# The seam between the MLP's last output product and the input-gradient product: a stated order of loads, and a first quarter with both halves over eight PSUM banks

## The chip, the cores and the metric

The kernel runs on one core of one Trainium2 chip. The metric is the time of one execution on the device in microseconds (us), the median of several runs. TensorE (PE in the profile) does the matrix products, VectorE (DVE) and ScalarE (ACT) the elementwise work, GpSimd (POOL) issues some of the DMAs and builds index tables, and SyncE (SP) issues most loads. [...] 

## The reference, cut to what matters

The forward pass is a conditioned mixer block, and the kernel returns its output and nine gradients for a given `grad_out`:

```
h = layernorm(x) * (1 + ca) + sa
x = x + ga * spectral(h)                  # rfft2, a learned filter, irfft2
h = layernorm(x) * (1 + cb) + sb
y = layernorm(h)
x = x + gb * (gelu(y @ w1 + b1) @ w2 + b2)
out, vjp = jax.vjp(forward, ...);  grads = vjp(grad_out)
```

There are S = 2048 tokens of D = 1024 features, and the MLP is F = 3584 wide; all inputs and outputs are bf16. With `ph` = (gb * grad_out) @ w2^T, the gradient at the MLP's hidden layer is `gz` = ph * gelu'(z), and the gradient at its input is gz @ w1^T. This last product is the one called the input-gradient product here. `sa` to `gb` are six rows of length D that come from `c` and `w_mod`; their gradients are sums over tokens, and the gradient of `w_mod` is an outer product of `silu(c)` with these sums.

## The kernel before, in words

The tokens are worked in NB = 4 blocks of BW = 512, and F in 7 groups g of 4 x 128 rows. The code is written as dataflow on named tiles. A scheduler puts the instructions of each engine in an order before the run, by priority and by when it reckons that tiles are free; `tc.issue_after(ins)` keeps an instruction behind `ins` in that order, `ordered()` keeps a PE instruction behind the PE instruction before it, and tiles with the same tag share a buffer, so that the later one waits for the earlier one's readers.

The stages around the change are these:

- `z_block(b, g0, g1)` (lines 782 to 817) computes z = y @ w1 (tile `pz`, L795), the gelu and its derivative, and stores `hh` (the activation) and `gz` to DRAM (L809, L817). It reads w1 from seven tiles with the tags `W1T`, and its temporaries `gt` take the tags t0 to t3.
- `bo_pass(b, h)` (L822) computes one half (512 of 1024 columns) of the MLP's output for block b in four PSUM banks `pbo`: a bias matmul each (L827), then 7 chunks of 16 matmuls (L836), each chunk against a slice of w2. The w2 slice is loaded by SP in the chunk's own program step (L831) into one of four buffers (w2sA, w2sC, w2sD, w2sB in turn). ACT then copies the banks out (L845), DVE multiplies and adds (L172, tile `otile`), the result is stored (L154, L159), and four narrow matmuls `pa` (L855) sum grad_out * output, which is added up in `gacc`.
- `plan` (L869 to 879) writes out the order of z blocks and bo chunks by hand. Blocks 0 to 2 have z blocks between the chunks; block 3 has none. The `pa` part of a pass is run one or two chunks into the next pass, and that of the last pass behind the loop (L898).
- Then come `pq` (L903), which finishes the sum in `gacc`, the store of its row (`store_gmod`, L178), and the gradient of b1 (`ptr`, L187, and L914).
- `gmod_ring` (L939) runs through w_mod row blocks with three buffers: load (L947), a product with sum (L958), a scaled row (L960), a store (L961). The instance `early` works on the row that `pq` made.
- `w1T_0` to `w1T_6` hold w1 transposed, 28 DMA transposes of 256 KB (L973) into the tags `W1T`. `gzr` are eight slots for gz (tags t0 to t3).
- The loop `for b in range(NB)` (L1001) does the input-gradient product: two halves h of 7 groups of 16 matmuls (`pg`, L1020) in four PSUM banks (`ps_f`), copied out by ACT with a running sum (L1025) into `gn3`. Then DVE takes the gradient through two layernorms (`ln_bwd`, L919 to 924; L1041), adds the residual, and folds the result for the spectral stage (`fold_tok`, `fold_d`, tiles n3u, pru, fbuf). `sums3` and `sums3_ga` (L195, banks `acc3a` and `acc3b`) add token sums on PE. The tile n3u is loaded once per block (L1005).
- Then the gradient of w2 begins (`gw2acc`, L1114); it needs four tiles `gB`, which take the buffers of w1T_0 to w1T_3 (load_tok, L127 and L130), and hh transposed from DRAM (`hht`, L1139).

Of the kernel before, what the change touches and what calls it, by code (L numbers as in the profile page):

```python
# [10 lines left out]
FP32 = mybir.dt.float32  # L11
BF16 = mybir.dt.bfloat16
I32 = mybir.dt.int32
ACT = mybir.ActivationFunctionType
# [3 lines left out]
P = 128  # L18
S = 2048
D = 1024  # L20
# [4 lines left out]
KH = D // 2  # L25
# [5 lines left out]
NB = 4  # L31
BW = S // NB
# [3 lines left out]
def kernel(  # L36
# [24 lines left out]
    nc = tc.nc  # L61
# [3 lines left out]
    small = ctx.enter_context(tc.tile_pool(name="small", bufs=2))  # L65
    reg = ctx.enter_context(tc.tile_pool(name="reg", bufs=1))
# [4 lines left out]
    W1T = PXT[2:6] + ["sma", "smb", "px0"]  # L71
# [7 lines left out]
    def ps_f(name):  # L79
        return psum.tile([P, 512], FP32, tag="f", name=name, bufs=4)  # L80
# [36 lines left out]
    d_gz_v = d_gz.rearrange("(fc p) s -> p fc s", p=P)  # L117
# [176 lines left out]
    wt = reg.tile([P, 2, NDC, 256], BF16, name="wt", tag="wt")  # L294
# [44 lines left out]
    for j in range(4):  # L339
        for cch in range(NDC):  # L340
# [326 lines left out]
    last_pe = [None]  # L667
# [80 lines left out]
    for g in range(7):  # L748
        wtile = reg.tile([P, NDC, BW], BF16, name=f"w1_{g}", tag=W1T[g])
# [11 lines left out]
    w2p = [uvp2[:, 1], reg.tile([P, 4, BW], BF16, name="w2sC", tag="gm")[:], px1t[:, 0]]  # L761
# [58 lines left out]
    w2n = [0]  # L820

    def bo_pass(b, h):  # L822
        cs_ = slice(h * KH, (h + 1) * KH)
# [2 lines left out]
            with ordered():  # L826
                last_pe[0] = nc.tensor.matmul(pbs[i][:], lhsT=ones_bf[0:1, :], rhs=b2_row[0:1, cs_], start=True, stop=False)  # L827
        for g in range(7):
            wp = w2p[w2n[0] % 4]
            w2n[0] += 1  # L830
            nc.sync.dma_start(out=wp, in_=w2_v[:, g * 4:(g + 1) * 4, cs_])  # L831
            hh = hh_slots[(b * 7 + g) % 11]
            for i in range(4):
                for k in range(4):
                    with ordered():
                        last_pe[0] = nc.tensor.matmul(pbs[i][:], lhsT=hh[:, k, i * P:(i + 1) * P], rhs=wp[:, k, :],  # L836
                                                      start=False, stop=(g == 6 and k == 3))
            if g < 6:
                yield
# [9 lines left out]
        store_tok_half(out_0, bo, b, h)  # L849

        yield
        pa = (ps_d if b < NB - 1 else ps_f)("pa")
        for i in range(4):
            with ordered():
                last_pe[0] = nc.tensor.matmul(pa[32 * i:32 * (i + 1), :], lhsT=ones_bf[:, 0:32], rhs=go[:, i, :], start=True, stop=True)  # L855
# [14 lines left out]
    bo_late = []  # L870
# [9 lines left out]
    for kind, b, g in plan:  # L880
# [7 lines left out]
        else:  # L888
# [6 lines left out]
                bo_late.clear()  # L895
            if g == 13:
                next(boq[b], None)
    for late in bo_late:  # L898
        next(late, None)
    g5 = []  # L900
    for h in range(2):
        pq = (ps_s, ps_d)[h]("pq")
# [62 lines left out]
                load_w(n + 2)  # L965
            yield

    w1Ts = []
    for g in range(7):
        wtile = reg.tile([P, 4, D], BF16, name=f"w1T_{g}", tag=W1T[g])  # L970
        for k in range(4):
            fc = g * 4 + k
            nc.sync.dma_start_transpose(out=wtile[:, k, :], in_=B_w1[:, fc * P:(fc + 1) * P])  # L973
        w1Ts.append(wtile)
    gzr = [reg.tile([P, 2, 4, BW], BF16, name=f"gzr{k}", tag=f"t{k}") for k in range(4)]
# [7 lines left out]
    gzn = 0  # L983
# [4 lines left out]
    au = reg.tile([P, 4, D], BF16, name="au", tag="px1")  # L988
# [9 lines left out]
    def sums3_ga(b, p4):  # L998
        halves_sum(acc3[1], p4, b == 0, b == 3)

    for b in range(NB):  # L1001
        gn3 = gn3s[b % 2]
        sums = small.tile([P, 2, 4], FP32, tag="sums")
        gzt = []
# [5 lines left out]
        for g in range(7):  # L1010
            sl = gzr[gzn % 8 // 2][:, gzn % 2]
            gzn += 1
            nc.sync.dma_start(out=sl, in_=d_gz_v[:, g * 4:(g + 1) * 4, b * BW:(b + 1) * BW])
            gzt.append(sl)
        for h in range(2):
            pgs = [ps_f("pg") for _ in range(4)]
            for g in range(7):
                for i in range(4):
                    for k in range(4):
                        nc.tensor.matmul(pgs[i][:], lhsT=gzt[g][:, k, i * P:(i + 1) * P],  # L1020
                                         rhs=w1Ts[g][:, k, h * KH:(h + 1) * KH],
                                         start=(g == 0 and k == 0), stop=(g == 6 and k == 3))
            for i in range(4):
                with tc.high_priority():
                    nc.scalar.activation(out=gn3[:, i, h * KH:(h + 1) * KH], in_=pgs[i][:], func=ACT.Identity,  # L1025
                                         accum_out=sums[:, h, i:i + 1])
        tt(sums[:, 0, :], sums[:, 0, :], sums[:, 1, :], ALU.add)
        for i in range(4):
            t = 4 * b + i
# [9 lines left out]
        for i in range(4):  # L1039
            t = 4 * b + i  # L1040
# [240 lines left out]
```

## Time and profile before

| what | value |
|---|---|
| median of 3 runs | 1520.55 us |
| the three runs | 1515.2 to 1523.6 us |
| the profiled execution: its own time | 1518.75 us |
| the profiled execution: span on the core | 1516.6 us |
| mean granted clock of TensorE in it | 0.98 |

A row of the timeline begins with the start in us from the beginning of the span and the time that the merged instructions took; then stand the engine, the line, the operation, what it writes and reads, and how many instructions were merged. Square brackets hold the idle time of that engine just before, and what released it. "SPq" is the time that SP took to issue a DMA, not the transfer. In a row of the windows stand the busy time of PE, weight loads, DVE, ACT and POOL, then the granted clock, the share of the DMA engines' time, and GB/s. Some matmul records are missing from a trace.

### The profile page before, as it was taken

To read this page: it belongs to the slowest core of one execution; us is meant where nothing else is said; L and a number is where in the kernel's file an instruction comes from. 1 tells how busy PE (TensorE), PEld (TensorE's weight loads), DVE (VectorE), ACT (ScalarE), POOL (GpSimd) and SP (SyncE) were. 2 spreads that over 40 slices of the span, in tenths; PEclk is the share of its full clock that TensorE was granted. 3 is DMA by queue.
4 is the path that set the end of the run, shared out by engine and by line. 5 is a ranking of instruction groups with operands and counts; after the bars stand their busy time and mean duration, and the time that the engine had idled before them with its cause. 6 is when DMAs were issued, how large, how long until landed. Compare 5 with 4: busy or idle time off the path is not lost.

```text
span 1516.6 us, 18226 instructions
## 1 busy us (share of the span) xinstructions
PE 1413.6 (93%) x6702; PEld 654.1 (43%) x6835; DVE 1070.0 (71%) x1575; ACT 724.6 (48%) x959; POOL 370.1 (24%) x427
## 2 busy tenths in 40 slices
PE   5899899999899999999889999969999899999998
PEld 2444445444344444444334444424444444444443
DVE  5883767897799887877313877958075775998633
ACT  4765556758787765666011423322622344443211
POOL 5710621210112122211112101321033331232333
PEclk8999999999999999999999999979999999999999
DMA  9882564999787776899956246398388976856994
GB/s 337 260 222 70 153 181 153 277 241 323 236 251 238 231 239 230 242 291 261 326 190 220 99 150 222 124 225 195 82 202 212 238 227 177 225 170 164 274 244 151
DMA packets 358168, 324.27 MB, mean 214 GB/s; under 512 B 209191, under 2 KB 300861, under 8 KB 357824
## 3 DMA queue, kind: packets, MB, share of 16 engines
q1 hardware_dynamic: 324192, 207.71, 51.3%
q0 software_dynamic: 33888, 115.41, 22.8%
q8 instruction: 53, 0.87, 0.2%
q14 instruction: 35, 0.29, 0.1%
HBM read 164.15 MB, written 109.10 MB: 180 GB/s over the span
## 4 chain that ended last, share of the span: by engine, by line
PE 49%; DVE 20%; issue 10%; DMA 10%; ACT 6%; POOL 4%; SPq 1%; POOLq 0%; ACTq 0%; DVEq 0%
PE pbo L836 10%; PE pz L795 10%; PE gw2acc L1114 9%; PE pg L1020 5%; PE gw1acc L1181 4%; PE pv L563 3%; DVE ct L172 3%; PE pu L470 3%; PE pp L678 2%; DVE got L919 2%; DVE fbuf L172 2%; PE po L628 1%; DVE gn3a L924 1%; DMA gB<-in_grad_out_dram 1%; ACT ct L460 1%
## 5 line engine op out<-in xcount | busy, mean ns | idle before, releaser
L678 PE MATMUL pp<-gBoT,wt 128*128 128x512 bf16 x876 | 198.4, 379 | 5.6 <-DMA wt<-in_B_w_dram 1.9
L1020 PE MATMUL pg<-w1T,gzr 128*128 128x512 bf16 x876 | 195.3, 381 | 1.5 <-issue 0.7
L1181 PE MATMUL gw1acc<-gzh,n3n 128*128 128x512 bf16 x876 | 194.7, 379 | 0.9
L795 PEld LDWEIGHTS <-w 128*128 128x128 bf16 x896 | 87.7, 98 | 111.3 <-issue 7.9
L1020 PEld LDWEIGHTS <-gzr 128*128 128x128 bf16 x896 | 87.2, 98 | 109.4 <-issue 7.2
L678 PEld LDWEIGHTS <-wt 128*128 128x128 bf16 x896 | 87.4, 98 | 106.3 <-issue 3.7
L1181 PEld LDWEIGHTS <-n3n 128*128 128x128 bf16 x896 | 87.4, 98 | 104.1 <-issue 1.3
L795 PE MATMUL pz<-n3Ta,w 128*128 128x512 bf16 x437 | 99.5, 383 | 5.0 <-ACT gt L798 4.2
L1114 PE MATMUL gw2acc<-gB,hhsA 128*128 128x512 bf16 x437 | 100.7, 383 | 1.2 <-DMA hhsA<-d_hh 0.4
L1119 ACT CAST gwo<-gw2acc 128x512 bf16<-128x512 f32 x54 | 30.8, 584 | 146.7 <-PE gw2acc L1114 94.8
L795 PE MATMUL pz<-n3Tb,w 128*128 128x512 bf16 x439 | 98.4, 379 | 0.5
L836 PEld LDWEIGHTS <-hhA 128*128 128x128 bf16 x608 | 59.0, 98 | 75.2 <-issue 5.2
L798 ACT ACTIVATE gt<-pz,b_col 128x512 bf16<-128x512 f32 x112 | 73.0, 683 | 34.4 <-PE pz L795 32.3
L804 ACT ACTIVATE gt<-gt 128x2048 bf16<-128x2048 bf16 x28 | 53.5, 1910 | 67.5 <-DVE gt L172 67.5
L172 DVE TENSOR_TENSOR gt<-gt,gt 128x2048 bf16<-128x2048 bf16 x56 | 68.5, 1223 | 21.6 <-ACT gt L806 20.9
L1185 ACT CAST gwo<-gw1acc 128x512 bf16<-128x512 f32 x49 | 28.3, 582 | 104.9 <-PE gw1acc L1181 91.5
L172 DVE TENSOR_TENSOR ct<-ct 128x2048 bf16<-128x2048 bf16 x64 | 76.0, 1219 | 3.2 <-ACT ct L631 1.9
L1114 PE MATMUL gw2acc<-gB,hht 128*128 128x512 bf16 x251 | 59.4, 396 | 14.3 <-DMA hht<-d_hh 10.3
L1114 PEld LDWEIGHTS <-hhsA 128*128 128x128 bf16 x448 | 44.1, 99 | 52.6 <-issue 2.7
L800 ACT ACTIVATE gt<-gt 128x2048 bf16<-128x2048 bf16 x28 | 53.4, 1907 | 0.6
L806 ACT ACTIVATE gt<-gt 128x2048 bf16<-128x2048 bf16 x28 | 53.4, 1907 | 0.5
L958 DVE CUSTOM_DVE_ANT_0 otl<-otl 128x1024 bf16<-128x1024 bf16 x16 | 19.1, 1223 | 43.6 <-DMA otl<-in_w_mod_dram 35.6
(313 smaller groups left out, 2521.1 us busy)
## 6 DMA issues: line engine op xcount, KB each, us to landing
gzr<-d_gz SPq DMA_DIRECT2D x28, 512.0 KB
wblk<-in_w_mod_dram SPq DMA_DIRECT2D x12, 1024.0 KB
d_ph<-pho POOLq DMA_DIRECT2D x21, 512.0 KB
out_dram<-otl POOLq DMA_DIRECT2D x40, 256.0 KB
d_hh<-hhA POOLq DMA_DIRECT2D x19, 512.0 KB
w2sD<-in_B_w_dram SPq DMA_DIRECT2D x14, 512.0 KB
hhC<-d_ph SPq DMA_DIRECT2D x14, 512.0 KB
w2sA<-d_ph SPq DMA_DIRECT2D x14, 512.0 KB
```

Of the source, the lines that this page charges most:

```text
L172: return nc.vector.tensor_tensor(out=out, in0=a, in1=b, op=op)
L470: last_pu[0] = nc.tensor.matmul(pu[:], lhsT=fb[:, i, cl, c8 * P:(c8 + 1) * P], rhs=sm[:, i, :], start=(i == 0), stop=(i == 3))
L678: last_pe[0] = nc.tensor.matmul(pp[:], lhsT=wt[:, fg % 2, cch, k * P:(k + 1) * P], rhs=gBoT[j][:, cch, :], start=(cch == 0), stop=(cch == ...
L795: last_pe[0] = nc.tensor.matmul(pz[:], lhsT=w1s[g][:, cch, k * P:(k + 1) * P], rhs=n3T[:, cch, :], start=(cch == 0), stop=(cch == NDC - 1))
L798: nc.scalar.activation(out=zb[:, k, :], in_=pz[:], func=ACT.Identity, bias=b1_col[:, fc:fc + 1], scale=1.0)
L800: nc.scalar.activation(out=av, in_=zb, func=ACT.Square)
L804: nc.scalar.activation(out=sg, in_=bv, func=ACT.Sigmoid, scale=2.0 * GK)
L806: nc.scalar.activation(out=bv, in_=bv, func=ACT.Sigmoid, scale=-2.0 * GK)
L836: last_pe[0] = nc.tensor.matmul(pbs[i][:], lhsT=hh[:, k, i * P:(i + 1) * P], rhs=wp[:, k, :], start=False, stop=(g == 6 and k == 3))
L1020: nc.tensor.matmul(pgs[i][:], lhsT=gzt[g][:, k, i * P:(i + 1) * P], rhs=w1Ts[g][:, k, h * KH:(h + 1) * KH], start=(g == 0 and k == 0), sto ...
L1114: nc.tensor.matmul(acc[:], lhsT=hh_s[hh_o[fc]][:, t, :], rhs=gBs[t // 4][:, t % 4, h * KH:(h + 1) * KH], start=(t == 0), stop=(t == NT - 1))
L1181: nc.tensor.matmul(acc[:], lhsT=n3ns[t // 4][:, t % 4, cch * P:(cch + 1) * P], rhs=gz2[t // 8][:, t % 8, :], start=(t == 0), stop=(t == NT ...
```

## The change

It changes four things.

1. The w2 loads get a function of their own, `w2_load(upto)`; in block 3 each chunk asks for three chunks ahead in the program.
2. The w1 transposes and the gz loads of block 0 are written out before the last `pa`, with a place relative to the w2 loads of block 3: transpose number fc (from 8 on) behind load fc - 8 of that block, the gz load of group g behind load 11 + g (at most the last).
3. Block 0 of the input-gradient product is taken out of the loop. Its two halves run interleaved, in the order h = 0, 0, 1, 0, 1, ..., 0, 1, 1 by groups, the first half in the four banks `ps_f`, the second in the four banks `ps_s` and `ps_d`. They stand behind the last bo chunk; the last `pa` follows after two groups, and `pq`, its row and b1's gradient come behind the block.
4. In the loop, `sums3_ga(b - 1)` stands behind the matmuls of block b instead of at the end of block b - 1. The buffers of gn3a and pru change places (uv0 and uv3), and the last `pa` but one uses `ps_f`, the last one `ps_d`.

The core of the diff:

```diff
+    def w2_load(upto):
+        while len(w2_in) <= min(upto, NB * 14 - 1):
+            n = len(w2_in)
+            h, g = n // 7 % 2, n % 7
+            w2_in.append(nc.sync.dma_start(out=w2p[n % 4], in_=w2_v[:, g * 4:(g + 1) * 4, h * KH:(h + 1) * KH]))
...
-            wp = w2p[w2n[0] % 4]
-            w2n[0] += 1
-            nc.sync.dma_start(out=wp, in_=w2_v[:, g * 4:(g + 1) * 4, cs_])
+            n = (2 * b + h) * 7 + g
+            w2_load(n + 3 if b == NB - 1 else n)
+            wp = w2p[n % 4]
...
-        pa = (ps_d if b < NB - 1 else ps_f)("pa")
+        pa = (ps_f if (b, h) == (NB - 1, 0) else ps_d)("pa")
...
-    for late in bo_late:
-        next(late, None)
...
+    def load_gz(b, g):
+        n = b * 7 + g
+        gzs[b, g] = gzr[n % 8 // 2][:, n % 2]
+        nc.sync.dma_start(out=gzs[b, g], in_=d_gz_v[:, g * 4:(g + 1) * 4, b * BW:(b + 1) * BW])
+
+    def behind_w2(k):
+        return tc.issue_after(w2_in[(NB - 1) * 14 + min(max(k, 0), 13)].ins)
+
+    for g in range(7):
+        wtile = reg.tile([P, 4, D], BF16, name=f"w1T_{g}", tag=W1T[g])
+        for k in range(4):
+            fc = g * 4 + k
+            with behind_w2(fc - 8) if fc >= 8 else ExitStack():
+                nc.sync.dma_start_transpose(out=wtile[:, k, :], in_=B_w1[:, fc * P:(fc + 1) * P])
+        w1Ts.append(wtile)
+        with behind_w2(11 + g):
+            load_gz(0, g)
...
+    def pg_pass(b, h, pool, before=lambda: ExitStack()):
+        pgs = [pool(k)("pg") for k in range(4)]
+        for g in range(7):
+            for i in range(4):
+                for k in range(4):
+                    with before():
+                        last_pg[0] = nc.tensor.matmul(pgs[i][:], lhsT=gzs[b, g][:, k, i * P:(i + 1) * P],
+                                                      rhs=w1Ts[g][:, k, h * KH:(h + 1) * KH],
+                                                      start=(g == 0 and k == 0), stop=(g == 6 and k == 3))
+                    last_pe[0] = last_pg[0]
+            if g < 6:
+                yield
...
+    pg0 = [pg_pass(0, 0, lambda k: ps_f, ordered), pg_pass(0, 1, lambda k: (ps_s, ps_d)[k // 2], ordered)]
+    for n, h in enumerate((0, 0, 1, 0, 1, 0, 1, 0, 1, 0, 1, 0, 1, 1)):
+        if n == 2:
+            for late in bo_late:
+                next(late, None)
+        next(pg0[h])
...
-    gn3s = [reg.tile([P, 4, D], BF16, name="gn3a", tag="uv0"), reg.tile([P, 4, D], BF16, name="gn3b", tag="wt")]
...
-    pru = reg.tile([P, 4, D], BF16, name="pru", tag="uv3")[:]
+    pru = reg.tile([P, 4, D], BF16, name="pru", tag="uv0")[:]
...
+        if b > 0:
             for g in range(7):
+                load_gz(b, g)
+            for h in range(2):
+                for _ in pg_pass(b, h, lambda k: ps_f):
+                    pass
+            with tc.issue_after(last_pg[0].ins):
+                sums3_ga(b - 1, au)
...
         if b < NB - 1:
-            sums3_ga(b, au)
             next(early, None)
```

In the built program, the order of instructions on every engine is the same as before up to the w2 loads of block 3 and from the first `gw2acc` on. The eight steps of `early` stand on DVE among the work of blocks 0 and 1 instead of ahead of it.

More of the change, by code (lines that the diff above doesn't have):

```diff
@@ L897, with gn3_of @@
                 next(boq[b], None)
-    for late in bo_late:
-        next(late, None)
+    w1Ts = []
+    gzr = [reg.tile([P, 2, 4, BW], BF16, name=f"gzr{k}", tag=f"t{k}") for k in range(4)]
+    gzs, g_sums, gn3s = {}, {}, {}
+    def gn3_of(b):
+        if b % 2 not in gn3s:
+            gn3s[b % 2] = reg.tile([P, 4, D], BF16, name=f"gn3{'ab'[b % 2]}", tag=("uv3", "wt")[b % 2])
+        return gn3s[b % 2]
+    def load_gz(b, g):
+        n = b * 7 + g
+        gzs[b, g] = gzr[n % 8 // 2][:, n % 2]
+        nc.sync.dma_start(out=gzs[b, g], in_=d_gz_v[:, g * 4:(g + 1) * 4, b * BW:(b + 1) * BW])
@@ new lines @@
+    last_pg = [None]
+    def pg_pass(b, h, pool, before=lambda: ExitStack()):
[10 more added lines that the diff above has]
+                yield
+        for i in range(4):
+            with tc.high_priority():
+                nc.scalar.activation(out=gn3_of(b)[:, i, h * KH:(h + 1) * KH], in_=pgs[i][:], func=ACT.Identity,
+                                     accum_out=g_sums[b][:, h, i:i + 1])
+        yield
@@ L982 @@
     acc3 = [ps_d("acc3a"), ps_d("acc3b")]
-    gzn = 0
     gmw = reg.tile([P, 2, D], BF16, name="gmw", tag="ph")
@@ L1001 @@
     for b in range(NB):
-        gn3 = gn3s[b % 2]
-        sums = small.tile([P, 2, 4], FP32, tag="sums")
-        gzt = []
+        if b > 0:
+            g_sums[b] = small.tile([P, 2, 4], FP32, name="sums", tag="sums")
+        sums = g_sums[b]
         nc.sync.dma_start(out=n3u[:], in_=chunk_rows(d_n3, b))
@@ L1009 @@
         load_tok(go4, grad_out, b)
[L1010 to L1016, printed above, removed]
-            for g in range(7):
[L1018 to L1026, printed above, removed]
+        if b > 0:
+            for g in range(7):
+                load_gz(b, g)
[4 more added lines that the diff above has]
+                sums3_ga(b - 1, au)
+        gn3 = gn3_of(b)
         tt(sums[:, 0, :], sums[:, 0, :], sums[:, 1, :], ALU.add)
```

11 lines of the change are left out of this document (2 added, 9 removed).

## The prediction

> **What bounds the kernel now.** I read the page first, then TensorE's timeline across the seam, then the queues that feed it. The page:
>
> ```profile
> PE 1413.6 (93%) x6702; PEld 654.1 (43%) x6835; DVE 1070.0 (71%) x1575; ACT 724.6 (48%) x959; POOL 370.1 (24%) x427
> ```
>
> TensorE is busy 93% of 1516.6 us, so a local edit can win little more than the gaps that TensorE has at its place. The order of the built program is the same in both kernels outside the seam and the four pg blocks; before and after them I expect only a shift. TensorE's timeline there:
>
> ```profile
> 709.03 3.62 PE L836 MATMUL pbo<-w2sA,hhA 128*128 128x512 bf16 x16
> ...
> 718.49 0.86 PE L827 MATMUL pbo<-b_row,ones_bf 1*128 1x512 bf16 x2 [1.85 <-ACT otile L845]
> ...
> 729.30 3.61 PE L836 MATMUL pbo<-w2sA,hhB 128*128 128x512 bf16 x15 [2.61 <-DMA w2sA<-in_B_w_dram]
> ...
> 737.07 3.61 PE L836 MATMUL pbo<-w2sD,hhA 128*128 128x512 bf16 x16 [0.70 <-DMA w2sD<-in_B_w_dram]
> ...
> 745.11 3.61 PE L836 MATMUL pbo<-w2sA,hhA 128*128 128x512 bf16 x16 [0.72 <-DMA w2sA<-in_B_w_dram]
> ...
> 753.54 3.61 PE L836 MATMUL pbo<-w2sD,hhB 128*128 128x512 bf16 x15 [0.29 <-DMA w2sD<-in_B_w_dram]
> 757.08 0.40 PE L855 MATMUL pa<-otile,ones_bf 128*32 128x512 bf16 x4
> ...
> 767.78 3.62 PE L836 MATMUL pbo<-w2sD,hhA 128*128 128x512 bf16 x16
> 771.24 3.62 PE L836 MATMUL pbo<-w2sB,hhA 128*128 128x512 bf16 x16
> 776.12 1.02 PE L903 MATMUL pq<-w2sD,quad 128*1 128x512 f32 x2 [1.27 <-ACT otile L845]
> ...
> 779.97 0.62 PE L855 MATMUL pa<-otile,ones_bf 128*32 128x512 bf16 x4 [2.64 <-DVE otile L172]
> 780.92 3.19 PE L1020 MATMUL pg<-w1T,gzr 128*128 128x512 bf16 x7 [0.33 <-issue]
> 784.04 1.86 PE L903 MATMUL pq<-w2sD,quad 128*1 128x512 f32 x2
> 785.84 50.52 PE L1020 MATMUL pg<-w1T,gzr 128*128 128x512 bf16 x229
> ```
>
> Three things stand in it. A w2 chunk of 16 matmuls takes 771.24 - 767.78 = 3.46 us, 0.216 each. Four chunks wait for their w2 load: 2.61 + 0.70 + 0.72 + 0.29 = 4.32 us. And from the last pbo (771.24 + 3.62 = 774.86) to the steady pg at 785.84 pass 10.98 us with 8 pg matmuls (one record is missing), the pa and the pq in them; the 7 of 780.92 take 0.43 us each instead of 0.216, behind an idle stretch. The wait of 1.85 is for ScalarE and stays.
>
> Why w2 is late, from the sync queue, the transposes of w1T and the 5 us windows (DMA share and GB/s end the row):
>
> ```profile
> 711.19 10.90 SPq L973 DMA_TRANSPOSE w1T<-in_B_w_dram  x4
> 722.82 0.45 SPq L831 DMA_DIRECT2D w2sA<-in_B_w_dram  x1
> ...
> 761.07 0.37 SPq L831 DMA_DIRECT2D w2sB<-in_B_w_dram  x1
> ```
>
> ```profile
> L973 SPq DMA_TRANSPOSE w1T<-in_B_w_dram x28: 1159/2069/3892, 625.2 to 718.8; - x28
> ```
>
> ```profile
> 660.00:680.00 20.00, 19.89 (x93) 8.64 (x94) 15.47 (x21) 11.70 (x13) 2.54 (x3) 1.00 0.97 275
> 730.00:735.00 5.00, 4.95 (x24) 2.27 (x24) 0.00 (x0) 0.00 (x0) 0.00 (x0) 1.00 1.08 370
> ```
>
> The w2 load that came 2.61 us late was issued at 722.82, behind four transposes that held the queue 10.90 us, though its slot's last readers (709.03 + 3.62) were done at 712.65.
>
> **The change, part by part.**
>
> *The stated order.* 20 of the 28 transposes and the seven gz loads of block 0 leave the stretch of 650 to 745 us and go behind w2 loads, one transpose per load; nine transposes and six gz loads go behind the last two. In a chunk's 3.46 us the queue then moves one w2 load (0.5 MB at 370 GB/s, 1.42 us) and one transpose (median 2.07 us): 3.49 us, even with TensorE, with stores and otile loads on top; each w2 load is due three chunks (10.4 us) after its slot comes free. Bounds: all 4.32 us won, or a like 4.3 us still lost. The nearest row is 660 to 680: the same mix at DMA share 0.97, and TensorE busy 19.89 of 20. I take **4.3 us won**. The last w2 load goes out at 761.07 - 4.32 = 757; behind it come 9 x 2.07 + 6 x 1.42 = 27.1 us, so the last gz lands near 784. The interleaved pass starts at 770.5 and needs its last group (g = 6) 11 chunks and the pa later, at 809: it is covered by 25 us.
>
> *The seam.* pg's first half uses banks that the pass before last left free; the four of the second half are free when ScalarE has copied the last pbo, two chunks later. So pg follows pbo without a gap, pa fits behind 32 matmuls (6.9 us, against 779.97 - 774.86 = 5.1 now, of which ScalarE's n2u work, now behind the copies, was a part), and pq with its transpose goes behind the block. Of 10.98 us remain 8 x 0.216 = 1.73 and pa 0.33: **8.9 us won** at the end of block 0's pg. Ends: 7.8 (if pq's 1.1 us delays someone there) and 8.9; pq now stands where TensorE must wait for VectorE anyway.
>
> So pg of block 0 ends 13.2 us earlier. What takes some of it back is VectorE:
>
> ```profile
> 777.18 0.68 DVE L177 CAST row<-pq 1x512 bf16<-1x512 f32 x1 [18.88 <-PE pq L903]
> ...
> 795.25 1.23 DVE L958 CUSTOM_DVE_ANT_0 gmw<-gmw,gmg 128x1024 bf16<-128x1024 bf16 x1 [8.62 <-DMA gmg<-d_gmod]
> ...
> 797.54 0.88 DVE L960 TENSOR_SCALAR gmw<-gmg,u_rt 128x1024 bf16<-128x1024 bf16 x2
> ...
> 821.12 0.88 DVE L960 TENSOR_SCALAR gmw<-gmg,u_rt 128x1024 bf16<-128x1024 bf16 x2
> 830.86 1.23 DVE L919 CUSTOM_DVE_ANT_0 got<-gn3a,n3u 128x1024 bf16<-128x1024 bf16 x1 [8.86 <-ACT gn3a L1025]
> ...
> 835.22 2.48 DVE L924 SCALAR_TENSOR_TENSOR gn3a<-gn3a,stats,got 128x1024 bf16<-128x1024 bf16 x2 [1.12 <-ACT got L923]
> ...
> 861.69 1.28 DVE L924 SCALAR_TENSOR_TENSOR gn3a<-gn3a,stats,got 128x1024 bf16<-128x1024 bf16 x1 [1.37 <-ACT got L923]
> ...
> 876.92 2.36 DVE L172 TENSOR_TENSOR fbuf<-pru 128x2048 bf16<-128x2048 bf16 x2
> 884.54 1.23 DVE L919 CUSTOM_DVE_ANT_0 got<-gn3b,n3u 128x1024 bf16<-128x1024 bf16 x1 [5.26 <-DMA n3u<-d_n]
> ```
>
> *The moved gmod ring.* It needs pq's row. Now its eight steps run from 795.25 to 822.0, beside block 0's pg, when VectorE is idle. With pq behind that pg, the built order puts seven products and six scalings of them into block 0's VectorE chain: at (797.54 - 795.25) / 2 = 1.15 and 0.88 / 2 = 0.44 that is 10.7 us, less the gap of 1.37 and one like that of 1.12 which they fill, 8.2 us; the casts of pq (2 x 0.68) stand in the gap of 1.12 and leave some 0.3. Now this chain runs 830.86 to 876.92, when n3u is read out, then VectorE waits 5.26 for the next n3u; from chain to chain 53.7 us, VectorE at work or in short gaps for 48.4. After: 48.4 + 8.5 = 56.9 by VectorE alone. n3u comes free behind five products and four scalings, at 46.1 + 0.3 + (5 x 1.15 + 4 x 0.44 - 2.5) = 51.4, and took 884.54 - 876.92 = 7.6 us to arrive, which gives 59.0. Chain 1 comes 3.2 to 5.3 us later than rigidly shifted; I take 5, since the queue of loads is as full as now.
>
> *The ga sums.* Their eight matmuls waited for VectorE in the middle of pg; they now stand behind the next block's pg, long ready:
>
> ```profile
> 869.88 0.61 PE L195 MATMUL acc3b<-au,ones_bf 128*32 128x512 bf16 x8 [1.09 <-DVE au L172]
> ...
> 890.13 0.39 PE L195 MATMUL acc3a<-gn3b,ones_bf 128*32 128x512 bf16 x2 [1.40 <-DVE gn3b L924]
> ...
> 977.58 0.62 PE L195 MATMUL acc3b<-au,ones_bf 128*32 128x512 bf16 x8 [1.15 <-DVE au L172]
> 978.13 14.63 PE L1020 MATMUL pg<-w1T,gzr 128*128 128x512 bf16 x65
> 1003.03 3.59 PE L1114 MATMUL gw2acc<-gB,hht 128*128 128x512 bf16 x8 [10.27 <-DMA hht<-d_hh]
> ...
> 1012.27 17.96 PE L1114 MATMUL gw2acc<-gB,hht 128*128 128x512 bf16 x75 [0.34 <-DVE gB L172]
> ```
>
> That frees some 1.7 us of TensorE per block, but there VectorE and n3u set the pace, so I count none of it. It also takes an au load (1 MB, 2.8 us at 370 GB/s) from ahead of the last gB loads, which the gw2 stage at 1012.27 waits for:
>
> ```profile
> 974.08 14.64 SPq L1139 DMA_TRANSPOSE hht<-d_hh  x1
> 988.82 0.52 SPq L1047 DMA_DIRECT2D au<-d_A  x1
> 989.43 4.27 SPq L127 DMA_DIRECT2D gB<-in_grad_out_dram  x2
> ```
>
> The start of gw2 hangs on block 2's chain, by got and the gB loads. Its lag is 5 from the ring less 0 to 2.8 from au: I take **2.5 us lost** (ends 0.4, from 3.2 - 2.8, and 5.3). Renamed buffers (gn3a, pru) cost nothing: their earlier readers are done two blocks before.
>
> **Sum:** -4.3 - 8.9 + 2.5 = -10.7 us. The profiled execution took 1518.75 us (span 1516.6 and 2.15 around it), so 1508; the median of the three runs, 1520.55, is 1.8 higher, which would give 1510.
>
> **The rivals.**
>
> *Transfers still late* (1512). The w2 loads share their queue with as many bytes as now, only later; if the four waits stay, 4.3 us are missing: 1512.3. For it: 1.42 + 2.07 leaves no room in 3.46. Against: the row of 660 to 680.
>
> *The ring holds the chain* (1524). Now the ring takes 822.0 - 795.25 = 26.8 us for 8 x 1.59 = 12.7 us of work, since each step waits for a buffer to be stored and loaded. If all 26.8 stand in the chain in place of 10.7, 16.1 more are lost: 1524. For it: the 8.62 wait. Against: in the new order the steps lie 3 to 15 us apart, with other work between. [...]
>
> *Slower: late transposes* (1530). The hht transpose of 512 KB (128 x 16 x 128 elements) held the queue 14.64 us, 7.3 us per 256 KB, the size of a w1T one. At that price the nine behind the last w2 load and the gz loads take 9 x 7.3 + 8.5 = 74 us, end at 831, and the last group stops TensorE from 809 for 22 us: 1508 + 22 = 1530. It decides once one costs over (809 - 757 - 8.5) / 9 = 4.8 us. Against: none of the 28 took over 3.89. [...]
>
> *More is won* (1504). The load of n3u is quick, VectorE finds all its gaps for the ring, so that chain 1 lags by 1, and gB comes 2.8 earlier: 1518.75 - 13.2 - 1.8 = 1503.8. For it: the order of the steps; against: the 7.6 us that n3u took.
>
> **How the numbers follow.** Forecast 0.58; transfers late 0.14; ring 0.12; slower 0.08; more won 0.08. Half a per cent is 7.6 us, about what a measurement of this kernel can tell from no change: faster is below 1511.2. The forecast's own ends are 1506 and 1512 (the tail's 0.4 to 5.3 us, and pq's 1.1 on top); 0.06 of its 0.58 lie above that. Faster: 0.52 + 0.08 = 0.60; same: 0.06 + 0.14 + 0.10 = 0.30; slower, with 0.02 of the ring case: 0.10. The range 1502 to 1518 leaves out the slower case and most of the ring's.
>
> **What would show it.** In the profile after: no DMA wait of pbo in its last two passes; pg directly behind pbo at 0.216 us each with pa inside; VectorE reaching block 1's first got 57 to 59 us after block 0's; gw2 starting some 10.7 us earlier; everything behind it shifted alike. Wrong would be: waits of pg for w1T or gzr, a wait of VectorE for gmw or gmg over 3 us, or a gw2 start that has not moved.

## The result, and the profile after

The changed kernel takes 1513.98 us, the median of 14 runs (1505.84 to 1524.74), against 1519.83 us for the kernel before (14 runs); the comparison gives a ratio of 0.9957, with a 95% interval of 0.9937 to 0.9977 (the quotient of the two medians would be 0.9962). In two later comparisons it was 0.9940 (0.9915 to 0.9964) and 0.9967 (0.9945 to 0.9989). So the change wins 5 to 9 us. The forecast was 1508, 10.7 us below the profiled execution. The sign is right, the size 2 to 6 us too large, and 1513.98 lies above 1511.2, which the prediction had set as its line for "faster".

The profiled execution is the fastest of the 14, 1505.84 us (span 1503.9), 12.9 us below the one before, so its length alone would flatter the change. The page:

```profile
PE 1410.2 (94%) x6701; PEld 654.1 (43%) x6835; DVE 1069.0 (71%) x1575; ACT 726.4 (48%) x959; POOL 364.7 (24%) x427
```

TensorE's work is the same (1410.2 us, 1413.6 before); its idle time fell from 103.0 to 93.7 us. What can be compared are stretches. I count each from one point that every kernel here has: the bias matmuls of the last pass but one, which wait 1.85 us for ScalarE (718.49 before). TensorE's timeline across the seam, to be set against that of before:

```profile
719.95 0.86 PE L833 MATMUL pbo<-b_row,ones_bf 1*128 1x512 bf16 x2 [1.85 <-ACT otile L851]
720.74 5.31 PE L842 MATMUL pbo<-w2sD,hhA 128*128 128x512 bf16 x16
...
729.77 3.63 PE L842 MATMUL pbo<-w2sA,hhB 128*128 128x512 bf16 x15
...
769.27 3.62 PE L842 MATMUL pbo<-w2sB,hhA 128*128 128x512 bf16 x16
772.73 7.07 PE L939 MATMUL pg<-w1T,gzr 128*128 128x512 bf16 x31
779.73 0.40 PE L861 MATMUL pa<-otile,ones_bf 128*32 128x512 bf16 x4
780.06 10.32 PE L939 MATMUL pg<-w1T,gzr 128*128 128x512 bf16 x46
```

No DMA wait is left in the two passes, and pg follows the last pbo without a gap, `pa` inside it. The four waits of before (4.32 us) and the seam of 10.98 us are gone. One new thing stands in the second row: the chunk behind the wait takes 5.31 us instead of 3.62. The loads that were put off, on the sync queue:

```profile
762.25 4.93 SPq L926 DMA_TRANSPOSE w1T<-in_B_w_dram  x1
...
767.85 7.28 SPq L926 DMA_TRANSPOSE w1T<-in_B_w_dram  x4
...
775.80 7.69 SPq L926 DMA_TRANSPOSE w1T<-in_B_w_dram  x4
783.53 0.58 SPq L916 DMA_DIRECT2D gzr<-d_gz  x1
```

The last gz load goes out at 783.53; the prediction had it landing near 784, and pg waits for none of them. The nine transposes held the queue for 4.93 + 7.28 + 7.69 = 19.9 us, 2.2 each, though the first alone took 4.93. Behind the seam, VectorE's chains (the first got of blocks 0, 1 and 2):

```profile
819.84 1.23 DVE L977 CUSTOM_DVE_ANT_0 got<-gn3a,n3u 128x1024 bf16<-128x1024 bf16 x1 [38.98 <-ACT gn3a L947]
...
878.91 1.23 DVE L977 CUSTOM_DVE_ANT_0 got<-gn3b,n3u 128x1024 bf16<-128x1024 bf16 x1 [3.28 <-DMA n3u<-d_n]
...
934.53 1.23 DVE L977 CUSTOM_DVE_ANT_0 got<-gn3a,n3u 128x1024 bf16<-128x1024 bf16 x1 [6.08 <-DMA n3u<-d_n]
```

and TensorE beside them, to the gw2 stage:

```profile
884.76 0.61 PE L195 MATMUL acc3a<-gn3b,ones_bf 128*32 128x512 bf16 x2 [5.54 <-DVE gn3b L982]
...
939.89 0.39 PE L195 MATMUL acc3a<-gn3a,ones_bf 128*32 128x512 bf16 x2 [3.50 <-DVE gn3a L982]
...
998.65 3.44 PE L1153 MATMUL gw2acc<-gB,hht 128*128 128x512 bf16 x8 [9.52 <-DVE gB L172]
1003.04 18.29 PE L1153 MATMUL gw2acc<-gB,hht 128*128 128x512 bf16 x82 [0.94 <-DVE gB L172]
...
1022.24 34.71 PE L1153 MATMUL gw2acc<-gB,hht 128*128 128x512 bf16 x157
```

Chain 1 comes 878.91 - 819.84 = 59.07 us behind chain 0 (53.68 before), and TensorE, which no longer waits for the ga sums, waits 5.54 and 3.50 us for gn3 instead. The row of 34.71 us, the first long stretch of gw2, is in every kernel; it is the last mark that I count to. In the second profile of the same changed kernel (1517.57 us) the same mark looks otherwise:

```profile
995.93 1.87 PE L1153 MATMUL gw2acc<-gB,hht 128*128 128x512 bf16 x4 [6.64 <-DMA hht<-d_hh]
1007.27 3.57 PE L1153 MATMUL gw2acc<-gB,hht 128*128 128x512 bf16 x8 [9.47 <-DVE gB L172]
...
1031.40 34.71 PE L1153 MATMUL gw2acc<-gB,hht 128*128 128x512 bf16 x160
```

The table has all kernels, in us behind the start of the wait's row (in the order 718.49, 719.95, 721.02, 719.12, 721.38, 720.62, 721.16, 719.17, 718.97, 719.89, 720.84, 721.61, 717.76, 718.88): the end of the last pbo, the three chains, and that mark. Gains are differences to the first row. The mark is not the end of the program: from it to the end of the span pass 481.7, 484.3 and 488.2 us in the three profiles of the changed kernel and 484.0 before, so that a gain at the mark is not yet a gain of the execution. Their whole spans are 12.7, 0.9 and 2.8 us shorter than that of before.

| kernel | last pbo ends | chain 0 | chain 1 | chain 2 | gw2 mark | ratio of runs to before (95%) |
|---|---|---|---|---|---|---|
| before | 56.4 | 112.4 | 166.1 | 220.1 | 314.2 | 1 |
| changed, first profile | 52.9 | 99.9 | 159.0 | 214.6 | 302.3 | 0.9957 (0.9937 to 0.9977) |
| changed, second | 53.0 | 99.9 | 159.0 | 214.7 | 310.4 | 0.9940 (0.9915 to 0.9964) |
| changed, third | 51.3 | 98.2 | 157.8 | 212.6 | 306.5 | 0.9967 (0.9945 to 0.9989) |
| order of loads alone | 51.3 | 106.0 | 160.3 | 214.8 | 308.2 | 0.9972 (0.9950 to 0.9995) |
| seam alone | 61.6 | 108.5 | 168.2 | 224.4 | 323.0 | 0.9978 (0.9954 to 1.0002) |
| pq early | 54.2 | 112.5 | 164.9 | 217.0 | 310.7 | 1.0007 (0.9983 to 1.0032) |
| ring behind the folds | 51.3 | 98.2 | 151.0 | 204.1 | 306.1 | 0.9963 (0.9933 to 0.9993) |
| hht held | 52.9 | 99.9 | 159.3 | 215.0 | 304.9 | 0.9959 (0.9934 to 0.9984) |
| both | 51.3 | 98.2 | 150.6 | 203.7 | 299.0 | 0.9912 (0.9881 to 0.9942) |
| both, second time | 51.3 | 98.2 | 151.1 | 204.2 | 301.4 | 0.9940 (0.9916 to 0.9964) |
| both, smA held too | 54.2 | 101.1 | 153.6 | 206.6 | 305.2 | 0.9959 (0.9934 to 0.9985) |
| ga sums at the old place | 52.9 | 99.9 | 161.5 | 216.1 | 315.5 | 0.9986 (0.9959 to 1.0013) |
| the same, second time | 51.3 | 98.2 | 159.7 | 214.2 | 308.0 | 1.0012 (0.9981 to 1.0043) |

### The profile page after: what moved, and what is told of

It reads as the page before. It is cut to its first block, busy times and chain, and to the rows that moved or that the text cites. A ratio compares the mean times of both kernels' runs of the same rounds, so it can differ in the third digit from the quotient of the medians.

```text
span 1503.9 us, 18220 instructions
## 1 busy us (share of the span) xinstructions
PE 1410.2 (94%) x6701; PEld 654.1 (43%) x6835; DVE 1069.0 (71%) x1575; ACT 726.4 (48%) x959; POOL 364.7 (24%) x427
## 3 DMA queue, kind: packets, MB, share of 16 engines
q1 hardware_dynamic: 324192, 207.71, 51.4%
## 4 chain that ended last, share of the span: by engine, by line
PE 61%; DVE 16%; DMA 7%; issue 7%; ACT 5%; POOL 2%; SPq 1%; POOLq 0%; ACTq 0%; DVEq 0%
PE pbo L842 12%; PE pz L795 10%; PE gw2acc L1153 10%; PE gw1acc L1220 9%; PE pg L939 7%; PE pv L563 4%; PE pp L678 3%; PE pu L470 3%; DVE ct L172 3%; PE po L628 1%; DVE got L977 1%; ACT ct L460 1%; DMA n3u<-d_n 1%; DMA d_n<-ct 1%; PE pcs L503 1%
## 5 line engine op out<-in xcount | busy, mean ns | idle before, releaser
L795 PEld LDWEIGHTS <-w 128*128 128x128 bf16 x896 | 87.7, 98 | 111.3 <-issue 7.9
L1153 PE MATMUL gw2acc<-gB,hht 128*128 128x512 bf16 x251 | 57.2, 386 | 10.7 <-DVE gB L172 10.5
L1225 POOL DMA_DIRECT2D out_dram<-gwo x56 | 30.5, 545 | 79.8 <-ACT gwo L1224 54.0
```

The lines of the kernel that those rows point to most:

```text
L795: last_pe[0] = nc.tensor.matmul(pz[:], lhsT=w1s[g][:, cch, k * P:(k + 1) * P], rhs=n3T[:, cch, :], start=(cch == 0), stop=(cch == NDC - 1))
L1153: nc.tensor.matmul(acc[:], lhsT=hh_s[hh_o[fc]][:, t, :], rhs=gBs[t // 4][:, t % 4, h * KH:(h + 1) * KH], start=(t == 0), stop=(t == NT - 1))
```

## The experiments

**The changed kernel again** (x_after, no edit; x_after2, the same).

> The changed kernel once more, as the yardstick of its neighbours. Theory A (the gain that the first trace shows in the stretch up to gw2, 10.7 us, is a property of the program): from TensorE's wait of 1.85 us for ScalarE ahead of the last two pbo passes to the steady gw2 matmuls 283 us again, against 294 in the kernel before; ratio 0.993. Theory B (part of it was luck of that one execution, above all the hht transpose that held the queue 6.28 us instead of 14.64): the stretch is 286 to 290 us, the transpose takes some 14 us, ratio 0.996 to 0.998.

> The changed kernel a third time, to be set against the kernel without the moved ga sums on one chip, and for a third profile of the same program. Theory D (what differs between its executions is GpSimd's last pair of gB gathers and the granted clock behind idle stretches, nothing ahead of block 2): chain 2 again starts 214.6 us behind the wait of 1.86 us, while gw2's steady part starts anywhere from 283 to 290 us behind it, the later the longer the gap ahead of that pair (2.6 us gave 283, 9.9 us gave 290); ratio 0.994 to 0.996.

Up to chain 2 the three profiles agree within 2.1 us, of which 1.7 is the chunk of 5.31 us, which the third does not have. From chain 2 to the gw2 mark they take 87.7, 95.7 and 93.9 us (before: 94.1). From the start of the wait's row to the steady gw2 they take 283.1, 290.2 and 285.1 us. So the main part of theory B holds: the 10.7 us of the first profile were in part luck. The cause that it named does not: the first hht transpose held the queue 8.01 us in the second profile and 5.72 in the third, not some 14, and gw2 came later in both than in the first, where it held the queue 6.28. On GpSimd, ahead of the last pair of gB gathers, in the first and in the second profile:

```profile
985.63 2.56 POOL L130 DMA_INDIRECT gB<-in_grad_out_dram,xu  x1 [2.58 <-PE pg L939]
```

```profile
994.10 2.56 POOL L130 DMA_INDIRECT gB<-in_grad_out_dram,xu  x1 [9.92 <-issue]
```

In the three profiles gaps of 2.6, 9.9 and 4.9 us go with 302.3, 310.4 and 306.5. That is D's order, but not a rule: the kernel with both edits, below, has 9.3 us of gap and 299.0.

**Order of loads alone** (x_order). Block 0's pg goes back into the loop; pq, ring and ga sums stand where they were before.

```
-    pg0 = [pg_pass(0, 0, ...), pg_pass(0, 1, ...)]   # and its loop
+    for late in bo_late: next(late, None)
...
-            with tc.issue_after(last_pg[0].ins):
-                sums3_ga(b - 1, au)
```

> Only the stated order of loads; block 0's pg stays in the loop, with pq, pa and the gmod ring where they were. If the prediction's steps are right: the four DMA waits of pbo in the last two passes are gone (-4.3 us), the seam stays at about 11 us, block 1's first got comes 53.7 us after block 0's, and gw2 starts 4 us earlier: ratio 0.997. Rival (the waits only move): pg of block 0 then waits for w1T or gzr in its first groups, some 4 us, and gw2 starts where it did: ratio 1.000.

TensorE behind the last pbo:

```profile
769.02 3.62 PE L842 MATMUL pbo<-w2sB,hhA 128*128 128x512 bf16 x16
...
777.09 23.27 PE L939 MATMUL pg<-w1T,gzr 128*128 128x512 bf16 x107
803.54 29.31 PE L939 MATMUL pg<-w1T,gzr 128*128 128x512 bf16 x129 [3.18 <-ACT gn3a L947]
```

The four waits are gone (last pbo 5.1 us earlier), pg waits for no w1T or gzr, and the runs give 0.9972, 4.3 us as expected, with an interval from 0.8 to 7.6. The rival falls in the form in which it was stated. But one part of the expectation failed: the seam did not stay at 11 us. From the last pbo (769.02 + 3.62 = 772.64) to the steady pg pass 4.45 us, and then TensorE waits 3.18 us for ScalarE ahead of the second half. ScalarE's n2u work, which stood ahead of its copies of pbo in the kernel before (774.36), now waits for a load that went out only behind the transposes that were put off (790.29), and stands ahead of its copies of pg. So a part of the waiting did move. Chain 0 comes 6.4 us earlier, 1.3 more than the last pbo.

**Seam alone** (x_seam).

```
-            w2_load(n + 3 if b == NB - 1 else n)
+            w2_load(n)
...
-            with behind_w2(fc - 8) if fc >= 8 else ExitStack():
+            with ExitStack():
```

> Only the seam: block 0's pg interleaved over eight banks, with pq behind it, the ring in block 0's chain and the ga sums moved, but the w1T transposes and gz loads issued as early as in the kernel before. If the steps are right: the waits of pbo stay at about 4.3 us, the seam falls from 11 us to 2, chain 1 lags 5 us, and gw2 starts 6 us earlier: ratio 0.996. Rival (the order of loads carries the change, since a seam without gaps only moves VectorE's lag): gw2 starts 0 to 2 us earlier, ratio 0.999.

```profile
735.23 5.93 PE L842 MATMUL pbo<-w2sA,hhB 128*128 128x512 bf16 x16 [6.40 <-DMA w2sA<-in_B_w_dram]
...
752.49 3.61 PE L842 MATMUL pbo<-w2sA,hhA 128*128 128x512 bf16 x16 [0.76 <-DMA w2sA<-in_B_w_dram]
...
760.89 3.61 PE L842 MATMUL pbo<-w2sD,hhB 128*128 128x512 bf16 x16 [0.27 <-DMA w2sD<-in_B_w_dram]
```

The waits are back (7.4 us; its profiled execution, 1534.62 us, is the longest of its twelve). From the last pbo to chain 0 pass 108.5 - 61.6 = 46.9 us, as in the changed kernel, and 56.0 before: the seam is worth 9.1 us, and the prediction had 8.9. The gains at chain 0 do not quite add: 6.4 for the order and 9.1 for the seam make 15.5, and the changed kernel has 12.5 to 14.2. At the end 3.3 us are left of it, in an interval that takes in none. With the 4.3 of the order alone, that makes 7.6, about what the whole change wins.

**pq early** (x_pq): pq and the store of its row behind the fourth group of the first half.

```
-    for n, h in enumerate((0, 0, 1, 0, 1, 0, 1, 0, 1, 0, 1, 0, 1, 1)):
+    for n, h in enumerate((0, 0, 0, 0, 1, 1, 1, 0, 1, 0, 1, 0, 1, 1)):
...
+        if n == 4:
+            g5 = [...]; store_gmod(g5, 5)
```

> The changed kernel with pq and the store of gmod's row 5 behind the fourth group of pg's first half instead of behind block 0's pg, so that the eight steps of the ring run beside block 0's pg again; the rest is as changed. If the ring in block 0's chain costs what the prediction says: block 1's first got comes about 54 us after block 0's instead of 59.1, TensorE's wait of 5.54 us for gn3b shrinks to under 2, and gw2 starts 2 to 5 us earlier than in the changed kernel: ratio to before 0.990 to 0.992. Rival (the start of gw2 hangs on the hht transposes and the gB loads, whatever the chain does): chain 1 comes earlier, but gw2 starts within 1 us of the changed kernel's.

VectorE:

```profile
813.07 1.22 DVE L1016 CUSTOM_DVE_ANT_0 gmw<-gmw,gmg 128x1024 bf16<-128x1024 bf16 x1 [20.98 <-DMA gmg<-d_gmod]
...
830.34 1.23 DVE L1016 CUSTOM_DVE_ANT_0 gmw<-gmw,gmg 128x1024 bf16<-128x1024 bf16 x1 [3.89 <-DMA gmw<-in_w_mod_dram]
...
832.91 0.88 DVE L1018 TENSOR_SCALAR gmw<-gmg,u_rt 128x1024 bf16<-128x1024 bf16 x2
833.70 1.22 DVE L977 CUSTOM_DVE_ANT_0 got<-gn3a,n3u 128x1024 bf16<-128x1024 bf16 x1
```

The chains follow one another in 52.4 and 52.0 us, as expected without the ring, but the runs win nothing (1.0007), for a reason that neither theory named and that the prediction had as a rival: here the ring holds the chain. The row's load lands only at 813, the ring stands ahead of the chain in VectorE's order, and so block 0's got starts at 833.70, 112.5 us behind the wait's row instead of 99.9; TensorE then waits 9.57 us for gn3a. VectorE's rows show it: ahead of the got stand waits for loads of the ring of 20.98, 3.69, 3.89 and 0.18 us, and the got itself starts right behind the ring's last scalings (832.91) with no wait of its own.

**Ring behind the folds** (x_ring): three steps behind the last fold of block 0, three behind that of block 1, two behind that of block 2.

```
-        next(early, None)          # at two places in the chain
...
-            next(early, None)
+            with tc.issue_after(fold2_in[b].ins):
+                for _ in range(3):
+                    next(early, None)
```

> The changed kernel with the ring's steps held back: three behind block 0's last fold, three behind block 1's, two behind block 2's, where VectorE waits for the next n3u; nothing else is moved. If the ring in block 0's chain is what makes chain 1 late (59.1 us behind chain 0 against 53.7 before): block 1's first got comes 53 to 55 us after block 0's, TensorE's wait of 5.6 us for gn3b is under 2, and chain 2 starts 5 to 7 us earlier than in the changed kernel, counted from the wait of 1.86 us. If the start of gw2 follows the chain: 5 us earlier, ratio to before 0.990. Rival (gw2 hangs on the gB gathers and the hht transposes): gw2 starts less than 2 us earlier, ratio 0.994.

```profile
870.18 1.23 DVE L977 CUSTOM_DVE_ANT_0 got<-gn3b,n3u 128x1024 bf16<-128x1024 bf16 x1 [0.30 <-DMA n3u<-d_n]
...
923.23 1.22 DVE L977 CUSTOM_DVE_ANT_0 got<-gn3a,n3u 128x1024 bf16<-128x1024 bf16 x1
```

```profile
875.77 0.39 PE L195 MATMUL acc3a<-gn3b,ones_bf 128*32 128x512 bf16 x2 [0.89 <-DVE gn3b L982]
...
982.48 1.89 PE L1153 MATMUL gw2acc<-gB,hht 128*128 128x512 bf16 x4 [5.58 <-DMA hht<-d_hh]
1000.04 1.86 PE L1153 MATMUL gw2acc<-gB,hht 128*128 128x512 bf16 x4 [15.67 <-DVE gB L172]
```

The first half is borne out: chain 1 comes 52.8 us behind chain 0, and chain 2 8.5 to 10.6 us earlier than in the changed kernel. And it is worth nothing: TensorE now stands 5.58 and 15.67 us for hht and gB, the gw2 mark moves to 306.1, among the three of the changed kernel, and the runs give 0.9963. Even the first gB load went out 8.3 to 10.6 us earlier than in the changed kernel, counted from the same wait, and the steady gw2 begins 283.1 us behind that wait, no earlier than in the changed kernel's first profile. The rival holds: the start of gw2 hangs on the transfers.

**hht held** (x_gb): a store of 64 bytes from gB's gathered rows, and the second hht transpose and later ones behind it.

```
+    held = nc.sync.dma_start(out=d_mark[:]..., in_=gBs[3][0:1, 2, 0:32])
-    with tc.issue_after(gb_in.ins):
+    with tc.issue_after(held.ins):
         fill(6)
```

> The changed kernel with the second hht transpose and those behind it held until the last gB load has landed, by a store of 64 bytes from its gathered rows that stands ahead of them in the sync queue. Theory C (the hht transpose of 16 to 18 us behind the gB loads starves GpSimd's gathers for gB, of which the last pair was issued 9.9 us late in the second profile of the changed kernel and 2.6 us late in the first): the gap ahead of that pair is under 4 us, VectorE's four gB products are over by 1000 us on the clock of the second profile instead of 1011, the held transpose takes under 10 us, and gw2 runs steadily 3 to 8 us earlier than there; ratio to before 0.988 to 0.992, with a smaller spread. Rival (gw2's second chunk then waits for its transpose instead): gw2acc waits for hht some 10 us and nothing is won.

**Both** (x_both, and again x_both2): the last two edits together.

> Both edits: the ring behind the folds and the hht transposes behind the landed gB. If the chain and the gathers are two limits of the same start, the two gains add or nearly so: gw2 8 to 13 us earlier than in the second profile of the changed kernel, ratio to before 0.985 to 0.989. If only one of them is the limit, the ratio is that of the better of the two alone.

> The kernel with both edits (ring behind the folds, hht transposes behind the landed gB) once more, since its neighbour with the smA loads held too gave 0.996 where this one gave 0.991. If both edits together beat the changed kernel, which gave 0.994 to 0.997 in three comparisons, the ratio is 0.989 to 0.993 again; if the first comparison was a lucky one, 0.994 to 0.997. In the profile chain 2 should again start 204 us behind the wait of 1.86 us, and the last pair of gathers go out 0.56 us behind VectorE's first gB product, 9 us late.

Holding hht alone gives 0.9959, no more than the changed kernel; its gw2 mark, 304.9, lies among the others. The gap ahead of the last pair of gathers is 3.97 us and no gw2acc waits for hht, so theory C's first sign is there and the rival's is not; but the changed kernel shows gaps of 2.6 to 9.9 us without the edit, so the trace does not show that the edit did it. VectorE's gB products end 282.6 us behind the wait's row, against 283.0 to 290.1, and gw2 then begins at a low granted clock (0.57 in the window of 1000 to 1005 us; the first 28 matmuls that the trace holds, from 999.45, take 8.61 us, 0.31 each, and the 63 from 1008.97 take 13.98, 0.22 each), so that nothing of it is left at the mark. The edit also holds more than it says: in this kernel and in the three below, the 64 bytes are stored 0.03 us behind the end of one of VectorE's gB products, so the transposes stand behind that product, and not only behind the landed load. Both together give 0.9912 and 0.9940, gw2 marks of 299.0 and 301.4, below all three of the changed kernel. The expected 0.985 to 0.989 was not reached. The results fit two limits on one start, each hiding what the other edit wins, but they do not show it: these are the lowest ratios of the study, yet over the changed kernel the lead is some 4 us, the interval of the second comparison overlaps with those of the changed kernel, and the next kernel, which has both edits too, gives 0.9959.

**smA held too** (x_best).

```
     for cl in (CE, SE, CO, SO):
-        nc.sync.dma_start(out=(smA2, smB2)[cl % 2][:, cl // 2], in_=d_SF[:, cl])
+        with tc.issue_after(held.ins):
+            nc.sync.dma_start(out=(smA2, smB2)[cl % 2][:, cl // 2], in_=d_SF[:, cl])
```

> As the kernel with both edits (ring behind the folds, hht transposes behind the landed gB), and the four loads of smA and smB are held behind the landed gB too; in the kernel with both edits these moved up into the place of the transposes and the last pair of gathers still came 9.3 us late. Theory C (whatever the sync queue sends right behind the gB loads holds GpSimd's gathers): the gap ahead of the last pair is under 4 us, the four gB products end 4 to 8 us earlier than in the kernel with both edits, ratio 0.985 to 0.989. Rival (the gap belongs to the gathers themselves, by their number or by the last one's own tile): the gap stays at 9 us and the ratio at 0.991.

The late gather of GpSimd, and VectorE's first gB product:

```profile
985.67 2.56 POOL L131 DMA_INDIRECT gB<-in_grad_out_dram,xu  x1 [9.38 <-issue]
```

```profile
985.11 2.29 DVE L173 TENSOR_TENSOR gB<-gB,rows 128x4096 bf16<-128x4096 bf16 x1 [8.51 <-DMA gB<-in_grad_out_dram,xu]
```

```profile
970.00:975.00 5.00, 4.09 (x4) 1.00 1.18 102
975.00:980.00 5.00, 0.99 (x2) 1.00 1.12 125
980.00:985.00 5.00, 0.00 (x0) 0.92 0.98 221
985.00:990.00 5.00, 4.02 (x3) 0.50 1.03 398
```

(The windows are GpSimd's: busy time, granted clock, DMA share, GB/s.) The sync queue issues nothing between 976.3 and 998.5, and the last pair of gathers is 9.38 us late all the same. So theory C falls in its form "whatever the sync queue sends behind the gB loads". The pair goes out 0.56 us behind the start of the first gB product, here and in every profile of the changed kernel; in this one that product had waited for the first gB to land, so that the landing seems to release both. Why that takes until 985 the windows show in part: the DMA engines are full (a share of 1.18 and 1.12) while they move 102 and 125 GB/s, and give 398 (1.03) once the pair is out. The first hht transpose, issued at 964.5, is a transfer of that time; that it is the cause was not tried, since no kernel here put it behind the gB loads, and this stays open.

**ga sums at the old place** (x_ga, and again x_ga2).

```
-            with tc.issue_after(last_pg[0].ins):
-                sums3_ga(b - 1, au)
...
         if b < NB - 1:
+            sums3_ga(b, au)
             next(early, None)
```

> The changed kernel with the ga sums at their old place in the middle of pg, which also puts au's load ahead of the last gB loads again. If the prediction is right that the moved sums are free and au's place is worth 0 to 2.8 us: three waits of acc3b for VectorE come back, 1.1 us each, gw2 starts 0 to 3 us later than in the changed kernel, ratio to before 0.994 to 0.997. Rival (au's load ahead of the gB loads had kept them from colliding with the hht transposes): gw2 starts earlier than in the changed kernel and the last gathers are not held; ratio 0.990 to 0.993.

> The changed kernel with the ga sums at their old place once more, beside the changed kernel itself. If the prediction is right that the moved sums are worth 0 to 2.8 us, its ratio lies 0 to 0.002 above that of the changed kernel. If the first comparison holds (0.9986 against 0.994 to 0.996), the sums are worth some 4 to 7 us, and the ratio lies 0.003 to 0.005 above it.

```profile
859.78 0.62 PE L195 MATMUL acc3b<-au,ones_bf 128*32 128x512 bf16 x8 [1.31 <-DVE au L172]
...
884.76 0.61 PE L195 MATMUL acc3a<-gn3b,ones_bf 128*32 128x512 bf16 x2 [6.34 <-DVE gn3b L982]
```

(The other two waits for au are 0.57 and 0.36 us.) Without this step the runs show no gain of the change: 0.9986 and 1.0012, mean 0.9999, against 0.9955 for the three of the changed kernel. The step is worth 0.0044 of 1520, 6.7 us; with the comparisons taken as independent (half widths of the two means 0.0021 and 0.0013), that is 3 to 10 us. On the traces chain 2 is 1.5 to 1.6 us later (like chunk with like: 216.1 against 214.6, 214.2 against 212.6), and au's load is back between the first hht transpose and the last gB loads:

```profile
979.55 0.91 SPq L1085 DMA_DIRECT2D au<-d_A  x1
980.55 6.56 SPq L127 DMA_DIRECT2D gB<-in_grad_out_dram  x2
```

What au's place costs stands in VectorE's gB products, here and in the kernel before:

```profile
1005.92 2.29 DVE L172 TENSOR_TENSOR gB<-gB,rows 128x4096 bf16<-128x4096 bf16 x1 [1.93 <-DMA gB<-in_grad_out_dram]
```

```profile
1007.72 4.49 DVE L172 TENSOR_TENSOR gB<-gB,rows 128x4096 bf16<-128x4096 bf16 x2 [3.98 <-DMA gB<-in_grad_out_dram]
```

The third product waits for SP's own gB load: 1.93 and 1.97 us in the two profiles of this kernel, 3.98 before and 3.96 with the order of loads alone, all with au ahead of the last gB loads. In no profile with au behind them does a product wait for SP's load; it waits for the gathers. So some 2 us may belong to au's place, which the prediction had priced at 0 to 2.8, and 1.5 us to what comes before chain 2. Where the other 3 us of the 6.7 go is not shown: from chain 2 to the gw2 mark pass 99.4 and 93.8 us, against 87.7 to 95.7, so the second of the two lies inside the spread of the changed kernel. Nor do the parts add up: the order of loads alone leaves the sums at their old place and wins 4.3 us. Why the seam and the moved ring cost that much beside it when the sums stay was not tried, and the difference (0.0027, half width some 0.003) is not clear of the noise.

## Why the prediction was right, and where its size was off

*The stated order.* Right: 4.3 us were predicted; the last pbo ends 3.4, 3.4 and 5.1 us earlier, and by itself the order wins 4.3 us (0.8 to 7.6). The spread of 1.7 us is the chunk behind the wait of 1.85 us, which took 5.31 us in the first two profiles, with a granted clock down to 0.61 and 0.52, and 3.63 in the third; told below.

*The seam.* Right: 8.9 predicted, 9.1 measured against the kernel before. Against the kernel with the order alone, whose stretch from the last pbo to chain 0 is already shorter, it is 54.7 - 46.9 = 7.8. Chain 0 comes 12.5 to 14.2 us earlier (13.2 predicted).

*The ring in block 0's chain.* Right: the predicted spacing of the chains was 59.0, the measured ones 59.1, 59.1 and 59.6; TensorE shows it as the wait of 5.54. The path is the predicted one too: n3u was reckoned to come free 51.4 us behind the chain's start and to take 7.6 to arrive; its load goes out 51.8 behind (871.62 - 819.84), and VectorE goes on 7.3 later. With the ring behind the folds the spacing is 52.8. The load of n3u in the changed kernel:

```profile
871.62 0.45 SPq L1053 DMA_DIRECT2D n3u<-d_n  x1
```

One part was missing: from chain 1 to chain 2 another 0.7 to 1.6 us are lost (934.53 - 878.91 = 55.62, against 54.06 before), so that at chain 2 the lead is 5.5 to 7.5.

*The tail: the step that was mis-sized.* "I take 2.5 us lost (ends 0.4 and 5.3)": the lag of 5 was to be halved by au's new place. Its mean on the three traces: the gw2 mark comes 11.9, 3.8 and 7.7 us earlier, 7.8 in the mean, where 13.2 - 2.5 = 10.7 stood; so 5.4 are lost, at the upper end. That leaves 7.8 us of gain at the mark, and the runs give 5.0, 6.5 and 9.1. What failed in the step is its path: "The start of gw2 hangs on block 2's chain, by got and the gB loads." The kernel with the ring behind the folds has that chain 8.5 to 10.6 us earlier and the first gB load with it, and gw2 starts no earlier than in the first profile. Between the first gB load and steady gw2 lies a stretch of DMA engines that are mostly full (in the second profile a share of 0.74 to 1.57 in the windows of 5 us from 970 to 1010, at 105 to 342 GB/s). It takes 36 to 43 us in the changed kernel (1003.04 - 966.92 in the first profile, 1011.21 - 968.06 in the second), so it differs by 7 us between executions of one program, and 46.6 in the kernel with the ring behind the folds, where it began earlier. What in it sets the length stays open. The first profile alone would have confirmed the forecast: there the steady gw2 stands 283.1 us behind the wait's row (1003.04 - 719.95) against 293.8 (1012.27 - 718.49), 10.7 us.

*The ga sums.* "so I count none of it": wrong. Counted at 0, with 0 to 2.8 for au, they are worth 3 to 10 us here. In the sum this was hidden, and there luck had a part: with the sums at their old place the runs show all of the 13.2 us lost again (to within some 3 us), where the prediction would have had 3.2 to 5.3 lost. The tail was priced too cheap and the moved sums too low, and the two errors cancel for the most part.

*The rivals.* Transfers still late, and late transposes, did not come: the nine behind the last w2 load took 2.2 us each, far from the mean of 4.8 that decides, though one took 4.93. The ring holding the chain came only with pq moved forward; in the changed kernel VectorE waits for no gmw or gmg. *More is won* did not come: chain 1 lags by 5.4 to 5.9, not by 1.

## What to carry to other kernels

A gain ahead of a stretch of transfers that fills the DMA engines need not be kept: with the ring behind the folds VectorE's chain and the first gB load came some 10 us earlier, the stretch (a DMA share of 0.65 to 1.77 in the windows of 5 us from 955 to 1005) took 46.6 us instead of 36 to 43, and nothing was won. Work in queue order was priced here by what stood behind it: the ring on VectorE (chain 1 came 59.1 us behind chain 0 with the ring in block 0's chain, 52.8 with the ring behind the folds), and perhaps one load on SP (VectorE waited 1.93 to 3.98 us for SP's gB load where au went ahead of it). A step that looks free beside the slower engine can decide whether the rest of a change pays. One profile of each kernel is not enough where the stretch in question spreads more than the effect: compare several, stretch by stretch.

## What the runs showed of the hardware

Behind the wait of 1.85 us the granted clock dropped in some profiles of the changed kernel and not in others. In the two windows of 3 us from 720 to 726 it was 0.82 and 0.61 in the first profile and 1.00 and 0.52 in the second, and the chunk behind the wait took 5.31 us in both; it took 3.63 in the third. In the kernel before, with the order of loads alone and with the ring behind the folds the clock was 1.00 in both windows, and the chunk took 3.63. The windows (us, PE busy, granted clock, DMA share, GB/s), in the first profile of the changed kernel and in the kernel with the order alone:

```profile
720.00:723.00 3.00, 2.88 (x11) 0.82 1.23 201
723.00:726.00 3.00, 3.00 (x10) 0.61 0.51 191
```

```profile
720.00:723.00 3.00, 1.50 (x6) 1.00 1.13 294
723.00:726.00 3.00, 3.00 (x15) 1.00 0.84 233
```

So 1.7 us hang on it; in the profiles of pq early and of smA held too the chunk takes 6.33 and 6.36. Between the full matmuls on both sides of the wait pass 3.2 us in the first profile of the changed kernel (717.57 to 720.74), with four narrow bias matmuls in them, and 3.2 in the kernel before (716.10 to 719.28), where the clock stayed at 1.00: the length of this stretch does not tell the two cases apart. What does, no run here shows.
